# Five attention visits per batch, given SyncE and GpSimd orders, and a new front, in a fused attention and feed-forward kernel

## Chip, cores, metric

One core of one Trainium2 chip. The metric is the device time of one execution in microseconds (us), as the median of repeated runs.

## The reference

```python
k_proj = einsum('ks,bhsd->bhkd', E, k);  v_proj = einsum('ks,bhsd->bhkd', F, v)     # 1024 keys -> 64
attn   = softmax(q @ k_proj^T / sqrt(64))
x      = (attn @ v_proj) put back as (8*1024 tokens, 512)
out    = (relu(x @ w_in) ** 2) @ w_out                                            # 512 -> 2048 -> 512
# q, k, v: 8 batches, 8 heads, 1024 tokens, head size 64, float32
```

## The kernel before

The kernel interleaves two pipelines in an order written by hand. While the feed-forward part of batch b runs, pieces of the attention of batch b+1 are put between its groups of matmuls. A batch has 62 groups. In batches 1 to 7 they run as first half (16 groups of `x @ w_in`, then 15 groups of the second product) and second half (the same again). The second product is formed from seven products of sums and differences of blocks, whose left operands VectorE makes (`operands`).

A table says ahead of which group each attention piece is issued. These are the tables of before:

```python
ORDERED = {PE, DVE, Activation}          # engines that run in program order; SyncE and GpSimd are left to a scheduler
PIECES = {                               # the attention of the next batch, for batches 2 to 7 ahead of group ...
    0: "transpose_q", 1: "copy_kp", 2: "copy_vp", 4: "copy_v_down",
    24: "scores 0, scores 1, exponentials 0", 25: "exponentials 1",
    27: "sums 0, values 0 0, reciprocals 0", 30: "values 0 1", 31: "normalize 0 0", 32: "normalize 0 1",
    47: "scores 2, scores 3, exponentials 2", 48: "exponentials 3",
    50: "sums 1, values 1 0, reciprocals 1", 53: "values 1 1", 54: "normalize 1 0", 55: "normalize 1 1",
}
BATCH_1 = {32: "project", 33: "copy_kp, transpose_q, copy_vp", 36: "copy_v_down", ...}   # cut
BATCH_2 = {**PIECES, 1: "", 2: "", 4: "", 9: "project", 10: "copy_kp", 11: "copy_vp", 14: "copy_v_down"}
```

`project` is the product of E with K and of F with V. Q of a batch, transposed (`qT`), and the projected K, transposed (`kT`), are made by DMA transposes through the crossbar, issued by SyncE. Q, K and V of each batch are loaded by GpSimd's queue. Each has one buffer, so the next Q load waits for the crossbar to have read this Q, and the next K and V loads wait for `project`:

```python
qkv_pool = tile_pool(name="qkv", bufs=1);  qt_pool = tile_pool(name="qt", bufs=1)
aps = tile_pool(name="aps", bufs=2, space=PSUM)      # two buffers for all attention products
def transpose_q(self): nc.sync.dma_start_transpose(out=self.qT[:], in_=self.Q[:]...)
def copy_kp(self):     ...; nc.sync.dma_start_transpose(out=self.kT[:], in_=self.kp[:]...)
```

The softmax here doesn't subtract the row's maximum and nothing guards it: scores larger than these inputs give would overflow.

## Time and profile before

| | before |
|---|---|
| median of three runs | 488.42 us (487.66 to 489.07) |
| span of the profiled run | 485.8 us |
| period of a steady batch (start of one to start of the next) | 57.60 us |
| PE idle inside steady batches | none |

The first lines of the profile's page of before (busy time, share of the span, number of instructions):

```profile
span 485.8 us, 8378 instructions
PE 472.6 (97%) x3614; PEld 292.3 (60%) x3614; DVE 315.4 (65%) x380; ACT 262.4 (54%) x414; POOL 33.2 (7%) x46
```

TensorE is the bound. The losses that the busy share does not show are between matmuls. This is the PE timeline of a steady batch of before (start in us, length in us, line, output and inputs, tile shape, count):

```profile
219.53 1.91 PE L461 MATMUL ps_y<-T,s 128*128 128x256 bf16 x16
221.37 0.63 PE L201 MATMUL ps_att<-qT,kT 64*64 64x512 bf16 x8
221.93 1.92 PE L461 MATMUL ps_z<-w_out,s 128*128 128x256 bf16 x16
...
224.65 0.41 PE L216 MATMUL ps_att<-expT,ones 64*32 64x512 bf16 x8
224.88 0.40 PE L216 MATMUL ps_att<-expT,vp 64*32 64x512 bf16 x8
225.21 1.05 PE L461 MATMUL ps_y<-T,s 128*128 128x256 bf16 x8
...
228.00 0.41 PE L216 MATMUL ps_att<-expT,vp 64*32 64x512 bf16 x8
228.34 1.05 PE L461 MATMUL ps_y<-T,hsq 128*128 128x256 bf16 x8
```

Full-array matmuls of 256 columns go at 0.109 us each, so the 16 that start at 219.53 would end at 221.28; the scores start at 221.37. The scores hold the array until 221.93, 0.56 us, where two passes of 512 columns at 0.216 us (the pitch of the `ps_h` matmuls in this trace) would be 0.43. A lone set of values (228.00) holds it for 0.34 us, where one pass is 0.22. So each visit of attention pieces costs about 0.09 us going in and 0.12 to 0.13 us coming out. The Trainium skill ("TensorEngine Tiling (Array Packing)", Key Properties) says that changing the tiling mode drains TensorE; this trace agrees and puts about 0.22 us on a visit. Before pays it six times per batch.

In batches 0 and 1 PE waits. These are the lines of before's PE waits that matter (total us, times, longest):

```profile
PE ps_att L201 <- DMA kT<-kp: 0.5, 1, 0.5
PE ps_att L286 <- DMA Q_sb<-in_q_dram: 0.4, 1, 0.4
...
PE ps_kv L176 <- DMA V_sb<-in_v_dram: 0.2, 1, 0.2
```

SyncE's timeline of before around batch 1 (start, length of the issue):

```profile
57.73 5.02 SPq L167 DMA_TRANSPOSE qT<-Q_sb  x1
62.81 1.25 SPq L185 DMA_TRANSPOSE kT<-kp  x1
...
79.29 12.77 SPq L167 DMA_TRANSPOSE qT<-Q_sb  x1
92.11 0.58 SPq L625 DMA_DIRECT2D out_dram<-o_sb  x1
92.79 0.41 SPq L631 DMA_DIRECT2D out_dram<-o_sb  x1
94.48 1.22 SPq L185 DMA_TRANSPOSE kT<-kp  x1
```

The transpose of Q of batch 1 issues for 5.0 us when alone; that of batch 2, at 79.29, issues for 12.8 us, because the loads of batch 2 run then. Those loads could start only when the crossbar had read Q of batch 1, as GpSimd's timeline shows (in brackets: idle before, and what ended it):

```profile
66.84 0.87 POOL L78 DMA_DIRECT2D Q_sb<-in_q_dram  x1 [34.43 <-DMA qT<-Q_sb]
```

### The profile page before, as it was taken

The numbers are of one execution on the slowest core, as the hardware profiler recorded it, in microseconds if no ns is written. First come the engines' busy times: TensorE is split into PE (matmuls) and PEld (weight loads), VectorE is DVE, ScalarE is ACT, GpSimd is POOL, SyncE is SP. The second block draws the span as 40 slices with busy tenths as digits, with TensorE's granted clock in tenths as the row PEclk, the third lists the DMA queues.
The fourth block names the chain that finished last, engine by engine and source line by source line (L and its number), as shares of the span: only waits on it lengthen the run. The fifth ranks groups of instructions, "written<-read, shape, count | busy, mean of one in ns | idle before, by whom it ended". The sixth has DMA issues, their size and how long they took to land.

```text
span 485.8 us, 8378 instructions
## 1 busy us (share of the span) xinstructions
PE 472.6 (97%) x3614; PEld 292.3 (60%) x3614; DVE 315.4 (65%) x380; ACT 262.4 (54%) x414; POOL 33.2 (7%) x46
## 2 busy tenths in 40 slices
PE   4899999999999999999999999999999999999997
PEld 2444677475574845757475665747557474666656
DVE  2478855566848568495765848566694856848383
ACT  2487445665727556355655467264672746645351
POOL 6330020010020000100010000200000000000000
PEclk9999999999999999999999999999999999999999
DMA  9999999997389124991149921893232102020202
GB/s 162 204 205 206 164 144 219 235 170 178 46 145 226 30 88 86 172 187 44 44 89 194 162 88 20 141 220 66 88 74 68 45 0 88 2 88 0 88 0 88
DMA packets 72501, 55.46 MB, mean 114 GB/s; under 512 B 33936, under 2 KB 64656, under 8 KB 72464
## 3 DMA queue, kind: packets, MB, share of 16 engines
q0 software_dynamic: 30336, 29.36, 38.5%
q1 hardware_dynamic: 42128, 25.56, 20.7%
q8 instruction: 28, 0.46, 0.4%
q14 instruction: 9, 0.07, 0.0%
HBM read 59.24 MB, written 16.78 MB: 156 GB/s over the span
## 4 chain that ended last, share of the span: by engine, by line
PE 85%; DMA 10%; ACT 2%; POOL 1%; issue 1%; DVE 0%; POOLq 0%; DVEq 0%
PE ps_h L441 39%; PE ps_y L461 23%; PE ps_z L461 11%; DMA V_sb<-in_v_dram 7%; PE ps_x L461 5%; DMA w_in<-in_moe_w_in_dram 2%; PE ps_att L216 2%; PE ps_kv L175 2%; PE ps_att L201 2%; DMA kT<-kp 1%; ACT h_relu L492 1%; PE ps_kv L176 0%; POOL K_sb L91 0%; DVE hsq L500 0%; ACT hsq L498 0%
## 5 line engine op out<-in xcount | busy, mean ns | idle before, releaser
L441 PE MATMUL ps_h<-xT,w_in 128*128 128x512 bf16 x1024 | 225.0, 379 | 0.2 <-DMA w_in<-in_moe_w_in_dram 0.2
L500 DVE TENSOR_TENSOR hsq<-h_relu 128x1024 bf16<-128x1024 f32 x123 | 150.2, 1222 | 67.4 <-ACT h_relu L492 66.8
L492 ACT ACTIVATE h_relu<-ps_h 128x512 f32<-128x512 f32 x256 | 150.6, 597 | 66.2 <-PE ps_h L441 65.7
L441 PEld LDWEIGHTS <-w_in 128*128 128x128 bf16 x1024 | 99.5, 98 | 118.2 <-issue 1.8
L461 PEld LDWEIGHTS <-s 128*128 128x128 bf16 x1024 | 98.4, 98 | 19.6 <-issue 8.1
L461 PEld LDWEIGHTS <-hsq 128*128 128x128 bf16 x768 | 73.2, 98 | 19.4 <-issue 3.0
L461 PE MATMUL ps_y<-T,s 128*128 128x256 bf16 x512 | 62.4, 273 | 0.1
L574 DVE TENSOR_TENSOR o_sb<-ps_z,p_b 128x512 f32<-128x512 f32 x16 | 11.1, 692 | 52.9 <-issue 25.7
L455 DVE TENSOR_TENSOR s<-hsq 128x1024 bf16<-128x1024 bf16 x64 | 43.6, 684 | 0.0
L570 ACT COPY o_sb<-ps_y 128x512 f32<-128x512 f32 x15 | 8.8, 585 | 55.4 <-PE ps_y L461 55.4
L235 DVE TENSOR_TENSOR xT<-ps_att,rs 128x1024 bf16<-128x1024 f32 x28 | 33.0, 1217 | 7.3 <-ACT rs L229 7.3
L461 PE MATMUL ps_y<-w_out,hsq 128*128 128x256 bf16 x256 | 34.5, 273 | 0.3 <-DVE hsq L500 0.3
L461 PE MATMUL ps_x<-w_out,hsq 128*128 128x256 bf16 x256 | 33.2, 273 | 0.0
L461 PE MATMUL ps_y<-T,hsq 128*128 128x256 bf16 x256 | 31.7, 272 | 0.0
L208 ACT ACTIVATE expT<-ps_att 128x1024 bf16<-128x1024 f32 x28 | 27.4, 1028 | 6.4 <-PE ps_att L201 6.4
L461 PE MATMUL ps_z<-T,s 128*128 128x256 bf16 x256 | 30.8, 273 | 0.0
L461 PE MATMUL ps_z<-w_out,s 128*128 128x256 bf16 x256 | 30.6, 273 | 0.0
L570 ACT COPY p_b<-ps_y 128x512 f32<-128x512 f32 (+1 forms) x17 | 9.5, 560 | 28.1 <-PE ps_y L461 28.0
L78 POOL DMA_DIRECT2D Q_sb<-in_q_dram x7 | 6.1, 876 | 263.2 <-DMA qT<-Q_sb 262.8
L574 DVE TENSOR_TENSOR o_sb<-ps_y,p_d 128x512 f32<-128x512 f32 (+1 forms) x17 | 11.2, 660 | 19.2 <-PE ps_y L461 19.2
L228 ACT ACTIVATE rs<-ps_att 128x1024 f32<-128x1024 f32 x14 | 14.3, 1023 | 14.6 <-PE ps_att L216 14.6
L455 DVE TENSOR_TENSOR s<-s,hsq 128x1024 bf16<-128x1024 bf16 x32 | 21.9, 687 | 0.5
(74 smaller groups left out, 239.3 us busy)
## 6 DMA issues: line engine op xcount, KB each, us to landing
out_dram<-o_sb SPq DMA_DIRECT2D x30, 512.0 KB, 3.3
K_sb<-in_k_dram POOLq DMA_DIRECT2D x7, 1024.0 KB, 17.3
V_sb<-in_v_dram POOLq DMA_DIRECT2D x7, 1024.0 KB, 22.4
Q_sb<-in_q_dram POOLq DMA_DIRECT2D x7, 1024.0 KB, 9.6
w_in<-in_moe_w_in_dram POOLq DMA_DIRECT2D x8, 256.0 KB, 13.7
w_out<-in_moe_w_out_dram POOLq DMA_DIRECT2D x4, 512.0 KB, 13.2
K_sb<-in_k_dram POOLq DMA_DIRECT2D x2, 512.0 KB, 7.8
V_sb<-in_v_dram POOLq DMA_DIRECT2D x2, 512.0 KB, 12.7
```

Source lines behind the costliest of these rows:

```text
L175: nc.tensor.matmul(ps[0:KP, :], lhsT=ET[:, i, :], rhs=kv[:, :, i, :], start=f, stop=l)
L201: nc.tensor.matmul(ps[o, bank, :], lhsT=self.kT[r, 2 * pr + j, :], start=True, stop=True, rhs=self.qT[r, NT * (2 * pr + j):NT * (2 * pr + ...
L208: nc.scalar.activation(e[:], self.ps["s", pr][:], AF.Exp, scale=SCALE)
L228: nc.scalar.activation(rs[:], self.ps["r", g][:], AF.Ln)
L235: nc.vector.tensor_tensor(out=self.xT[:, 2 * g + e].rearrange("p a n t -> p a (n t)"), in0=self.ps["v", g, e][:], in1=self.rs[g][:], op=AL ...
L441: nc.tensor.matmul(ps[:], lhsT=w_in_blk(cb, fb), rhs=xT[:, cb, :, 2 * ch:2 * ch + 2], start=(cb == 0), stop=(cb == NCB - 1),)
L455: nc.vector.tensor_tensor(out=s[o][:, js], in0=x, in1=y, op=op)
L461: nc.tensor.matmul(ps[tb] if len(ps) == 2 else ps[0][:, tb], lhsT=lhs[:, j, tb * P:(tb + 1) * P], rhs=rhs[:, j], start=first and n == 0 an ...
L492: nc.scalar.activation(r[:, n], ps[:], AF.Relu)
L500: multiply = lambda: nc.vector.tensor_tensor(out=o, in0=r[:], in1=r[:], op=ALU.mult)
L570: nc.scalar.copy(to[:, t], ps)
L574: nc.vector.tensor_tensor(out=to[:, t], in0=ps, in1=more[:, t], op=ALU.add)
```

## The change

Its intent: five visits per batch instead of six, a reordered front (batch 0's second Q transpose, batch 1's and batch 2's pieces), SyncE and GpSimd in program order, and Q's transpose half a batch earlier, so that its buffer is free sooner.

```diff
-ORDERED = {PE, DVE, Activation}
+ORDERED = {PE, DVE, Activation, Pool, SP}
 PIECES = {
-    0: "transpose_q", 1: "copy_kp", 2: "copy_vp", 4: "copy_v_down",
-    24: "scores 0, scores 1, exponentials 0", 25: "exponentials 1",
-    27: "sums 0, values 0 0, reciprocals 0", 30: "values 0 1", 31: "normalize 0 0", 32: "normalize 0 1",
-    47: "scores 2, scores 3, exponentials 2", 48: "exponentials 3",
-    50: "sums 1, values 1 0, reciprocals 1", 53: "values 1 1", 54: "normalize 1 0", 55: "normalize 1 1",
+    1: "copy_kp", 2: "copy_vp", 4: "copy_v_down",
+    20: "scores 0, scores 1, exponentials 0", 21: "exponentials 1",
+    23: "sums 0, values 0 0, reciprocals 0", 26: "normalize 0 0",
+    28: "scores 2, scores 3, exponentials 2", 29: "exponentials 3",
+    47: "values 0 1, sums 1, reciprocals 1", 48: "normalize 0 1",
+    53: "values 1 0, values 1 1", 54: "normalize 1 0", 55: "normalize 1 1",
 }
 BATCH_1 = {
-    32: "project", 33: "copy_kp, transpose_q, copy_vp", 36: "copy_v_down", ...
+    33: "project", 34: "copy_kp, transpose_q, copy_vp", 37: "copy_v_down", ...      # five visits too; cut
-BATCH_2 = {**PIECES, 1: "", 2: "", 4: "", 9: "project", 10: "copy_kp", ...}
+BATCH_2 = {**PIECES, 1: "", 2: "", 4: "", 9: "project", 10: "copy_kp, transpose_q", ...}
-    9: "second_half 1 0, second_half 0 1",              # batch 0
+    9: "second_half 1 0", 10: "second_half 0 1",
@@ operands of the second product, batches 1 to 7 @@
-    operands(1, range(4))                   # right after the last square
+    operands(1, (0,))
@@ def p2a(): @@
+    if b: operands(1, (1, 3, 2))            # the other three after the second product
@@ batch loop @@
+    order K, V, Q for batch 1, else Q, K, V
+    if b and n == 33 and ahead: ahead.transpose_q()
```

GpSimd's instructions come out in the same order in both builds. SyncE's do not: before issues qT of batch 1 ahead of kT; the changed kernel issues kT of batch 1 ahead of qT.

## The prediction

> **What bounds it.** TensorE. The busy table gives PE 97% of a 485.8 us span at a granted clock of 0.999; VectorE is at 65%, ScalarE at 54%. The timeline shows batches 2 to 6 repeating every 57.60 us with no PE idle (stage table). The change removes no matmul, so a gain can come only from (a) time lost between matmuls in steady batches and (b) PE waits in batches 0 and 1.
>
> **Steady batches.** In the PE timeline each attention piece put between full-array matmuls costs about 0.09 us going in and 0.13 us coming out: four-quadrant scores take 0.56 us against 0.43 for two 512-column passes; a lone set of values takes 0.34 against 0.21. The Trainium skill ("TensorEngine Tiling (Array Packing)", Key Properties) says that changing the tiling mode drains TensorE; the trace agrees, about 0.22 us per visit. Before has six visits per batch, after five: 0.22 us saved. The scores now ahead of the last x product of the first half also hide the 0.08 us for which the next product waited on a VectorE addition. Estimate: 0.25 to 0.3 us for each of batches 1 to 6, about 1.6 us. The deferred operand sums, Q's transpose half a batch earlier and the loads are off the critical path there: loads land many us before the projection reads them in both.
>
> One tight place, checked with trace durations (exponential 1.03, Ln+Exp 2.1, copy 0.58): the copy that frees ps_y now follows the reciprocals and ends about 0.05 us before PE needs it. No stall, little margin.
>
> **Batch 0.** Three PE waits should shrink: 0.40 us for the second Q load (its transpose moves one step later), 0.24 us for V at the projection (moved behind one product), 0.51 us for kT before the first scores, because kT now leaves before qT on SyncE's queue instead of behind its 5.0 us issue. Together 1.1 us. In its last half ScalarE now does four exponentials and both reciprocals in one run, and sums, values and a ps_y product wait for them: I estimate 0.5 to 0.8 us of new waits, against 0.5 us for fewer visits. Net about 1.1 us.
>
> **Batch 1.** kT and qT of batch 2 are now issued back to back after the projection; before, qT was issued 15 us earlier (79.3 us, 12.8 us long among the loads). Alone it takes 4.7 us to issue and 6.7 to 7.3 us to land, so it lands just when the first scores, now four groups earlier, want it: I estimate 0.2 us of new wait (0 to 0.7).
>
> GpSimd's instruction order is the same in both builds; naming it changes nothing by itself.
>
> **Sum.** 1.6 + 1.1 - 0.2 = 2.5 us: 488.4 to **485.9 us**, range 484.3 to 487.4. Chances: faster by over 2% 1%, within 2% 98%, slower by over 2% 1%.
>
> **What will show it.** Steady batches of 57.3 us with five visits. First scores of batch 1 near 65.4 us instead of 66.7, no longer waiting for kT. The first scores of batch 2 wait at most some tenths on qT, whose issue shrinks from 12.8 to about 5 us. PE idle falls by about 1 us.
>
> **What would make it wrong.** qT of batch 2 landing late (over 1 us of PE wait near 101 us); the tight ps_y copy giving a repeated stall of 0.3 us per batch, which would cancel the steady gain; SyncE in program order holding back output stores until VectorE or ScalarE block.

## The result

| | before | changed |
|---|---|---|
| median, same session (4 runs each) | 488.04 us (487.65 to 489.07) | 488.24 us (487.64 to 489.00) |
| ratio | | 1.0002 (0.9979 to 1.0024) |
| span of the profiled run | 485.8 us | 487.2 us |
| period of a steady batch | 57.60 us | 57.38 us |
| first full product (`ps_h`) starts | 19.90 us | 21.80 us |

A ratio is the mean time of one kernel's fast runs over the mean of the other's in the same rounds, so it is not quite the ratio of the medians quoted; the brackets hold the 95% interval. The time lies outside the predicted range of 484.3 to 487.4.

The page, and the PE timeline of a steady batch of the changed kernel:

```profile
span 487.2 us, 8379 instructions
PE 472.1 (97%) x3614; PEld 293.3 (60%) x3614; DVE 313.5 (64%) x380; ACT 263.0 (54%) x414; POOL 33.1 (7%) x46
```

```profile
220.28 0.63 PE L204 MATMUL ps_att<-qT,kT 64*64 64x512 bf16 x8
...
223.56 0.41 PE L219 MATMUL ps_att<-expT,ones 64*32 64x512 bf16 x8
223.78 0.40 PE L219 MATMUL ps_att<-expT,vp 64*32 64x512 bf16 x8
...
228.59 0.70 PE L204 MATMUL ps_att<-qT,kT 64*64 64x512 bf16 x8
...
245.76 0.41 PE L219 MATMUL ps_att<-expT,vp 64*32 64x512 bf16 x8
245.99 0.40 PE L219 MATMUL ps_att<-expT,ones 64*32 64x512 bf16 x8
...
250.79 0.63 PE L219 MATMUL ps_att<-expT,vp 64*32 64x512 bf16 x16
```

There are five visits now (220.28, 223.56, 228.59, 245.76, 250.79; the last is followed by the projection), and the period is 0.22 us shorter, the cost of one visit. PE's waits and SyncE's and GpSimd's timelines, as for before:

```profile
PE ps_att L204 <- DMA qT<-Q_sb: 1.3, 1, 1.3
PE ps_kv L179 <- DMA V_sb<-in_v_dram: 1.1, 1, 1.1
PE ps_k L254 <- DMA K_sb<-in_k_dram: 1.1, 1, 1.1
```

```profile
58.40 1.30 SPq L188 DMA_TRANSPOSE kT<-kp  x1
59.82 4.84 SPq L170 DMA_TRANSPOSE qT<-Q_sb  x1
...
84.51 0.37 SPq L636 DMA_DIRECT2D out_dram<-o_sb  x1
85.96 0.37 SPq L642 DMA_DIRECT2D out_dram<-o_sb  x1
97.43 1.19 SPq L188 DMA_TRANSPOSE kT<-kp  x1
98.81 4.83 SPq L170 DMA_TRANSPOSE qT<-Q_sb  x1
```

```profile
68.69 0.87 POOL L81 DMA_DIRECT2D Q_sb<-in_q_dram  x1 [34.93 <-DMA qT<-Q_sb]
```

Two things are new in them. The first scores of batch 1 wait 1.3 us, now for qT, where before they waited 0.5 us for kT. And the projection of batch 2 waits 1.1 us for V: its first K product starts at 93.01, its first V product at 94.47. A third is only apparent: the loads of batch 2 start at 68.69 instead of 66.84 and qT issues at 59.82 instead of 57.73, but this whole run started later. The first full product of before and of the changed kernel:

```profile
19.90 0.82 PE L441 MATMUL ps_h<-xT,w_in 128*128 128x512 bf16 x3 [0.20 <-DMA w_in<-in_moe_w_in_dram]
```

```profile
21.80 0.81 PE L448 MATMUL ps_h<-xT,w_in 128*128 128x512 bf16 x3 [0.42 <-DVE xT L344]
```

Counted from there the loads of batch 2 start after 46.9 us in both, and the other traces of the two kernels have 46.4 to 47.1 (before) and 46.9 (changed). SyncE's new order did not delay them. The wait for K in the list above, at 9.6 us, is in the very first stage, which is the same in both kernels.

### The profile page after: what moved, and what is told of

It is laid out like the page before. It is cut to its first block, busy times and chain, and to the rows that moved or that the text cites. A ratio compares the mean times of both kernels' runs of the same rounds, so it can differ in the third digit from the quotient of the medians.

```text
span 487.2 us, 8379 instructions
## 1 busy us (share of the span) xinstructions
PE 472.1 (97%) x3614; PEld 293.3 (60%) x3614; DVE 313.5 (64%) x380; ACT 263.0 (54%) x414; POOL 33.1 (7%) x46
## 3 DMA queue, kind: packets, MB, share of 16 engines
q1 hardware_dynamic: 42128, 25.56, 20.2%
## 4 chain that ended last, share of the span: by engine, by line
PE 86%; DMA 8%; ACT 2%; DVE 1%; issue 1%; POOL 0%; POOLq 0%
PE ps_h L448 42%; PE ps_y L468 21%; PE ps_z L468 11%; PE ps_x L468 5%; DMA V_sb<-in_v_dram 5%; PE ps_kv L178 2%; PE ps_att L219 2%; DMA K_sb<-in_k_dram 2%; DMA qT<-Q_sb 2%; PE ps_att L204 1%; ACT h_relu L499 1%; PE ps_k L254 1%; DVE hsq L507 1%; ACT expT L307 0%; DVE xT L344 0%
## 5 line engine op out<-in xcount | busy, mean ns | idle before, releaser
L583 DVE TENSOR_TENSOR o_sb<-ps_z,p_b 128x512 f32<-128x512 f32 x16 | 11.1, 692 | 48.1 <-ACT p_b L579 25.1
L468 PE MATMUL ps_y<-T,hsq 128*128 128x256 bf16 x256 | 30.7, 272 | 0.0
L579 ACT COPY p_b<-ps_y 128x512 f32<-128x512 f32 (+1 forms) x17 | 9.4, 554 | 23.3 <-PE ps_y L468 23.2
L462 DVE TENSOR_TENSOR s<-hsq,s 128x1024 bf16<-128x1024 bf16 x32 | 21.8, 682 | 0.0
L579 ACT COPY p_a<-ps_y 128x512 f32<-128x512 f32 (+1 forms) x17 | 9.4, 561 | 19.3 <-PE ps_y L468 19.3
```

Of the source, the lines that this page charges most:

```text
L462: nc.vector.tensor_tensor(out=s[o][:, js], in0=x, in1=y, op=op)
L468: nc.tensor.matmul(ps[tb] if len(ps) == 2 else ps[0][:, tb], lhsT=lhs[:, j, tb * P:(tb + 1) * P], rhs=rhs[:, j], start=first and n == 0 an ...
L579: nc.scalar.copy(to[:, t], ps)
L583: nc.vector.tensor_tensor(out=to[:, t], in0=ps, in1=more[:, t], op=ALU.add)
```

## The experiments

Traces were compared at four points: the start of the first full product, the span less that start (which takes out most of the luck of the first loads), the wait for V at the projection of batch 2, and the time from the first to the last packet of batch 2's Q, K and V loads, read from the DMA records. The table holds every trace but e3's, whose loads come in another order; "front" says whose SyncE order and first tables the kernel has.

| trace | front | first full product, us | span less that | loads of batch 2, us | wait for V there, us |
|---|---|---|---|---|---|
| before, first | before | 19.90 | 465.9 | 22.2 | 0 |
| b1_before | before | 19.87 | 466.8 | 22.9 | 0.49 |
| b2_before | before | 19.95 | 466.1 | 22.6 | 0 |
| b3_before | before | 21.23 | 465.6 | 22.5 | 0 |
| e4_five_deferred | before | 20.75 | 464.1 | 22.0 | 0 |
| e4b_five_deferred | before | 21.05 | 464.8 | 21.9 | 0 |
| e2_five_only | before | 21.28 | 469.9 | 21.7 | 0 |
| e8_five_gate_later | before, projection later | 19.87 | 470.7 | 22.0 | 0 |
| changed, first | changed | 21.80 | 465.4 | 23.3 | 1.06 |
| a0_after | changed | 20.13 | 464.0 | 22.3 | 0 |
| a1_after | changed | 22.33 | 464.0 | 22.1 | 0 |
| a2_after | changed | 21.09 | 465.3 | 23.8 | 0.99 |
| e1_qT_first | changed, qT first | 21.07 | 465.5 | 23.8 | 0.69 |
| e5_kT_on_PE | changed, kT on PE | 19.85 | 464.3 | 22.2 | 0 |
| f1_front_only | changed | 19.89 | 467.1 | 23.9 | 1.13 |
| e6_Q_first_kT_PE | changed, Q first, kT on PE | 20.89 | 465.9 | 21.5 | 0 |
| e7_after_gate_later | changed, projection later | 19.98 | 464.4 | 24.1 | 0 |
| e9_stores_late | changed, stores later | 20.72 | 464.0 | 19.9 | 0 |
| e10_stores_late_kT_PE | as e9, kT on PE | 20.09 | 463.5 | 20.2 | 0 |

### The changed kernel again (a0_after, a1_after, a2_after)

No edit.

> The changed kernel again, unedited, for a tight ratio and a second trace. Theory T (the front is bound by a DMA chain: Q of batch 1 landed, its crossbar transpose, then the three loads of batch 2, then the projection of batch 2; kT issued ahead of qT lengthens it): ratio 0.998 to 1.002, and a wait for V of 0.7 to 1.5 us at the projection of batch 2 again, whatever the start. Rival L (the first look was an unlucky start, 1.9 us late at the first full product): ratio 0.995 to 0.997, and with a normal start no wait for V there.

> The changed kernel once more, with two of its relatives on one chip. Theory V (its runs split by whether V of batch 2 lands before the projection of batch 2): times from 485.8 to 489, in the trace a wait for V at that projection if the run is over 487.5 us and none if it is under 486.7; ratio 0.996 to 1.000. Rival L (only the start varies): runs of the changed kernel and of five visits with deferral spread alike.

> The changed kernel once more, for its start: span less the start of the first full product is 464.0 to 465.5 us whatever the start; before's is 465.5 to 467.

Measured: a0 486.26 us median (485.90 to 488.71) against 488.18, ratio 0.9967 (0.9946 to 0.9988). a1 487.53 (486.22 to 488.49) against 488.35, ratio 0.9978 (0.9960 to 0.9995). a2, one look, 488.18. The first result was thus a set of four from the slow end of the spread. Over all 17 runs of the changed kernel the mean is 487.46 us, over the 37 of before in those sessions 488.28, 0.17% apart.

Theory T held that the wait for V comes whatever the start: it failed, since a0 and a1 have none. Theory V held that every slow run has that wait: it failed too, since a1's traced run took 488.08 us without it, with the latest start of all, 22.33 us. What is left is two pieces of luck: the start, and V. The span less the start is 464.0 us without the wait for V and 465.3 to 465.4 with it.

### Before again, for its starts (b1_before, b2_before, b3_before)

No edit.

> The kernel before, unedited, for a second trace. Theory G (after the first repeats: a run's time is set by two pieces of luck, the landing of the very first K and V loads and the landing of V of batch 2 at the projection of batch 2; before reaches that projection just as V lands): a start 1 us later than the first trace of before makes it about 1 us longer in all, and the projection of batch 2 waits for V by under 0.5 us, unlike the changed kernel in its slow runs (1.1 us).

> Before once more, for its start. If starts are luck: the first full product anywhere from 19.8 to 22.4 us, and the span longer by most of the excess over 19.9. If the late start is the changed kernel's: 19.8 to 20.1 again.

> Before a fourth time, for its start. If starts are luck: the first full product anywhere from 19.8 to 22.4 us, with the span longer by most of the excess over 19.9. If the late start is the changed kernel's: 19.8 to 20.1 again.

Measured: 488.48, 487.85 and 488.60 us, one look each. b3 starts at 21.23 us: late starts fall on before too. The instructions of all engines up to there are the same in both kernels; starts in traces with before's front run from 19.87 to 21.28 us (the last in e2 below), with the changed front from 19.85 to 22.33. So the 1.9 us by which the changed kernel's first trace started late is not shown to be its own doing, though the samples are too small to exclude a small share.

### Q's transpose ahead of K's (e1_qT_first)

```diff
-    33: "project", 34: "copy_kp, transpose_q, copy_vp",
+    33: "project, transpose_q", 34: "copy_kp, copy_vp",
```

> The changed kernel with qT of batch 1 ahead of kT on SyncE's queue, nothing else. Theory T: qT issues at about 58 us instead of 59.8, lands near 67 instead of 68.7, the loads of batch 2 start 1.5 to 2 us earlier, the wait for V at projection 2 falls from 1.1 us to under 0.4, the first scores wait about 1 us (now for kT), and the time falls by 0.8 to 1.6 us: ratio 0.997 of before. Rival S (the new ScalarE order in the last half of batch 0 costs what the steady batches give): no change from the changed kernel, ratio 1.000.

Measured: 486.72 us median (486.08 to 488.37) against 488.18, ratio 0.9962 (0.9947 to 0.9978), with a0 at 0.9967 beside it on the same chip: no difference. Its traced run is its slowest. There the first scores waited 1.37 us for kT instead of qT, and V was still waited for. Exchanging two transposes on one queue exchanges which of them the scores wait for. Theory T's gain of 0.8 to 1.6 us did not come. It rested on the loads of batch 2 having been late; after the first full product they start at 47.1 us here, no earlier than the 46.9 of the changed kernel.

### Five visits without the deferred sums (e2_five_only)

Before, with only the new `PIECES` (and `transpose_q` kept at group 0).

```diff
 PIECES: the five-visit table of the change, with 0: "transpose_q"
```

> The kernel before with only the five-visit table for batches 2 to 7, its SyncE order and first batches as before. All theories: steady batches of 57.38 us instead of 57.60. Theory T and S: the front is as in before, so 1.1 to 1.4 us less in all, ratio 0.997 to 0.998. If the ratio is 1.000, the steady gain is given back somewhere after batch 2 and both are wrong.

Measured: 492.90 us median (492.67 to 497.32) against 488.18, ratio 1.0107 (1.0079 to 1.0136): 5 us slower, where all theories said 1.2 faster. PE's waits in its trace:

```profile
PE ps_att L216 <- DVE xT L235: 5.2, 6, 0.9
```

Six batches, 0.9 us each. The values pieces of one visit need both buffers for attention products (`aps`), and the first is free only when `normalize 0 1` has read it. VectorE runs in program order, and without the deferral five operand sums, one every 0.60 us, stand between its last square and that normalize (247.37 to 250.50 us of this trace). The deferral puts three of them behind it.

### Five visits with the deferred sums (e4_five_deferred, e4b_five_deferred)

```diff
 PIECES: as in e2
-    operands(1, range(4))
+    operands(1, (0,))
 def p2a():
+    if b: operands(1, (1, 3, 2))
```

> The kernel before with the five-visit table and with the operand sums of the second half put off until after the second product; SyncE order and the first batches' tables as before. If the missing deferral is what cost five visits alone 0.88 us per batch at the values piece, that wait is gone, the period is 57.38 us, and the kernel is 1.2 to 1.7 us faster than before (ratio 0.9965 to 0.9975), as fast as the changed kernel: then the front edits give nothing net. If the SyncE order or the load order matters in steady batches, the period stays at 57.6 or above.

> The kernel before with five visits and deferred sums, again, on the chip of the others. Theory V: it reaches the projection of batch 2 half a microsecond later after its start than the changed kernel and its Q load starts 0.3 to 1.9 us earlier, so it seldom waits there: 486.2 to 487.3, narrower than the changed kernel, ratio 0.9955 to 0.9975. Rival L: as wide as the changed kernel.

Measured: e4 486.34 us median (486.16 to 487.29) against 488.26, ratio 0.9960 (0.9945 to 0.9975). e4b 487.02 (485.98 to 491.56) against 488.35, ratio 0.9984 (0.9953 to 1.0014). The waits of e2 are gone and the period is 57.38 us in both traces. So the deferral, which the prediction called off the critical path, is what makes five visits possible, and these two edits alone give about as much as the whole change (e4b is not clear of noise). That e4b would be narrower than the changed kernel was wrong: it has a run of 491.56 us, whose trace was not taken. In its traced run (487.59 us) the first scores of batch 2 waited 0.56 us for kT, which was issued at 95.44 us and landed 8.6 us later; e8 below explains this. Nor did its Q load start 0.3 to 1.9 us earlier, as theory V had it: 46.8 us after the first full product, against 46.9.

### The front without the five visits (f1_front_only)

The changed kernel with before's six-visit table and without the deferral.

```diff
 PIECES: the table of before, without 0: "transpose_q"
-    if b and n == 33 and ahead: ahead.transpose_q()
+    if b and n == 48 and ahead: ahead.transpose_q()
-    operands(1, (0,)) ... operands(1, (1, 3, 2))
+    operands(1, range(4))
```

> The changed kernel with its front (batch 1's table, the reordered first stages, SyncE's and GpSimd's order, the projection and transposes of batch 2) and the old six visits without deferral. If the front is off the critical path or gives back what it saves: ratio 0.999 to 1.001, batches of 57.6 us from batch 2 on. If the front's 1.1 us is real: ratio 0.997 to 0.998.

Measured: 488.72 us median (488.22 to 489.99) against 488.00, ratio 1.0020 (1.0007 to 1.0033). The front by itself is 0.2% slower, outside both ranges that the expectation named. In its trace:

```profile
PE ps_att L204 <- DMA qT<-Q_sb: 1.2, 1, 1.2
PE ps_kv L179 <- DMA V_sb<-in_v_dram: 1.1, 1, 1.1
```

Two waits, 1.2 us for qT of batch 1 and 1.1 us for V of batch 2, against before's 0.5 us for kT, and no wait for V in three of before's four traces.

### K and V of batch 2 ahead of Q (e3_kv_before_q)

```diff
-    order = K, V, Q if b == 1 else Q, K, V
+    order = K, V, Q if b in (1, 2) else Q, K, V
```

> The changed kernel with batch 2 loaded as K, V, Q, so that K and V do not wait behind Q for the crossbar transpose of batch 1. Theory T: V of batch 2 lands before 85 us and projection 2 does not wait; but the transposes of batch 1 now run among loads, qT takes about 12 us to issue instead of 4.8, the first scores wait 4 to 8 us, and the kernel is 2 to 6 us slower than before (ratio 1.004 to 1.012). If transposes are not slowed by loads, it is 1 us or more faster than the changed kernel.

Measured: 497.56 us median (496.18 to 499.07) against 488.18, ratio 1.0186 (1.0166 to 1.0207). The loss of 9 us is half as much again as the most that was expected (6 us). PE's wait and SyncE's transposes:

```profile
PE ps_att L204 <- DMA qT<-Q_sb: 10.6, 1, 10.6
```

```profile
57.81 1.78 SPq L188 DMA_TRANSPOSE kT<-kp  x1
59.71 15.01 SPq L170 DMA_TRANSPOSE qT<-Q_sb  x1
```

With loads on the DMA engines the transpose of Q issues for 15.0 us instead of 4.8. This shows why Q comes first: its load waits for the crossbar and holds K and V back with it. The loss is more than the wait: batch 0 took 11.1 us more than in the changed kernel (74.47 us from the first full product to the start of batch 1, against 63.34), of which the longer wait is 9.2 to 9.5. The granted TensorE clock was 0.50 from 70.7 us, during the wait, to 80.9 us, 4.0 us after PE had resumed. The Trainium skill ("DMA: Bandwidth & Descriptors", Issuing engines are not separate DMA queues) says that DMAs of all issuing engines run on the same 16 DMA engines and interleave; the trace fits this: with GpSimd's loads under way SyncE's transpose took 15.0 us to issue, against 4.8.

### The projection of batch 2 later (e7_after_gate_later, e8_five_gate_later)

```diff
 e7 (changed kernel):  BATCH_2: ... 2: "transpose_q", 12: "project", 13: "copy_kp", 14: "copy_vp", 16: "copy_v_down"
 e8 (e4_five_deferred): BATCH_2: ... 12: "project", 13: "copy_kp", 14: "copy_vp", 16: "copy_v_down"
```

> The changed kernel with the projection of batch 2 three groups (2.6 us) later and the transpose of its Q issued early, before it. Theory V: no wait for V at that projection in any trace, the slow runs of the changed kernel go: all runs within 485.5 to 487.3, ratio 0.995 to 0.9965. If the transpose of Q still runs when kT is wanted, the first scores of batch 2 wait and the ratio is 0.998 or more. Rival L: spread as the changed kernel, and the same mean.

> Five visits with deferral on the front of before, and the projection of batch 2 three groups later. Theory V: equal to or up to 0.5 us faster than without the move (ratio 0.995 to 0.9965), since it hardly waits there. If kT of batch 2 now lands after 102.5 us, its first scores wait and it is slower by up to 2 us.

Measured: e7 489.57 us median (486.21 to 491.74) against 488.35, ratio 1.0025 (0.9995 to 1.0055). e8 492.96 (492.35 to 493.83) against 488.35, ratio 1.0092 (1.0077 to 1.0107). In e8:

```profile
PE ps_att L201 <- DMA kT<-kp: 4.6, 2, 4.2
```

```profile
98.01 2.02 SPq L185 DMA_TRANSPOSE kT<-kp  x1
```

```profile
107.28 0.76 PE L201 MATMUL ps_att<-qT,kT 64*64 64x512 bf16 x8 [4.17 <-DMA kT<-kp]
107.98 3.40 PE L462 MATMUL ps_z<-T,s 128*128 128x256 bf16 x16
```

On before's front Q of batch 2 is transposed early, so the loads of batch 3 start early (their first packet is at 96.4 us here), and a kT issued at 98.01 is caught among them: the scores got it at 107.28, 9.3 us later, and waited 4.2 us (the other of the two waits is the one in batch 1). The wait again cost more than itself: from 107.6 to 111.1 us the granted clock was 0.51, and the 16 matmuls at 107.98 took 3.40 us where they take 1.91 in a steady batch. This is what the changed front guards against, by issuing kT and qT together ahead of those loads, and it is a likely cause of e4b's slow run, which no trace shows. For e7 only its fastest run was traced, and that has no wait for V, as expected, though V landed 72.9 us after the first full product, later than the 71.2 at which the changed kernel's four traces reach that projection: the move hid a late V. What made four of the other five 2.5 to 5.5 us slower stays open. There is a hint: three of them, and e4b's slow run, show a mean granted clock of 0.995 or 0.996, e8's five runs 0.993 to 0.996, one run of before (490.86 us) 0.993, and the changed kernel's own runs 0.999 or 1.000. So these slow runs, too, probably held a long PE wait.

### Batch 1's kT off the crossbar (e5_kT_on_PE, e6_Q_first_kT_PE)

```diff
 e5:  33: "project, transpose_q", 34: "copy_kp_only, copy_vp", 37: "copy_v_down",
+     39: "transpose_k 0", 41: "transpose_k 1",       # eight small TensorE transposes and two copies
 e6:  batch 1 loaded Q, K, V;  31: "transpose_q", 39: "project", 40: "copy_kp_only, copy_vp",
      42: "copy_v_down", 43: "transpose_k 0", 44: "transpose_k 1"
```

> The changed kernel with kT of batch 1 made by eight TensorE transposes, so that only qT uses the crossbar there. Theory G with the DMA chain: qT issues when Q has landed, lands near 66.5 us; the first scores wait under 0.5 us instead of 1.05 to 1.34; loads of batch 2 start about 2 us earlier, no wait for V at projection 2 in any run; 0.5 to 1 us faster than the changed kernel's fast runs and 2 us faster than its slow ones: ratio 0.993 to 0.996. If the chain is not what binds, ratio as the changed kernel, 0.9965.

> As the last, and batch 1 is loaded Q, K, V with qT issued as soon as Q lands, among the loads, and the projection of batch 1 six groups later. Theory: qT takes 12 us or more to issue but has landed by 60 us; the loads of batch 2 start near 60 us, 7 to 9 us earlier; no wait at the first scores or at projection 2; ratio 0.992 to 0.996. If V of batch 1 now lands after 59 us, projection 1 waits for it and the gain is lost.

Measured: e5 487.71 us median (485.89 to 488.03) against 488.26, ratio 0.9977 (0.9959 to 0.9995). e6 489.19 (488.24 to 490.30), ratio 1.0017 (0.9999 to 1.0035). In e5's traced run, its fastest, the first scores waited 0.25 us and V was not waited for, as expected, but four of its six runs took 487.5 us or more, so the expectation for "any run" cannot be upheld. Nor did the loads of batch 2 start earlier (47.0 us after the first full product, against 46.9). And the first scores came no earlier: 46.5 us after the first full product, as in the changed kernel; only the waiting had been filled. In e6 the loads of batch 2 started 42.3 us after the first full product, 4.6 earlier than in the changed kernel, but V of batch 1, now last, made projection 1 wait 1.85 us, the case its expectation named as a loss.

### The two stores held back (e9_stores_late, e10_stores_late_kT_PE)

With SyncE in program order the two 512 KB stores that end batch 0 go out at 84.51 and 85.96 us, in the middle of the loads of batch 2. Before held them, by accident, behind the 12.8 us issue of qT until 92.11. e9 is the changed kernel with these stores issued after qT of batch 2; e10 adds e5's edit.

```diff
 # batch 0, second half
-    nc.sync.dma_start(out_rows[...], o_tile)
+    late.append(lambda: nc.sync.dma_start(out_rows[...], o_tile))
 # batch 1, group 10, after copy_kp and transpose_q
+    while late: late.pop(0)()
```

> The changed kernel with the two stores of batch 0's second half issued after the transposes of batch 2 instead of at 83 to 86 us. Theory W (the stores share the DMA engines with the loads of V and delay it): the loads of batch 2 take 22.3 us or less, no wait for V at projection 2, and the slow runs go: ratio 0.995 to 0.997, all runs under 487.5. If the stores are not the cause: the wait of about 1 us in half the traces and the ratio 0.997 to 0.999 as for the changed kernel.

> The same with kT of batch 1 made on TensorE, so that qT of batch 1 and with it the loads of batch 2 start up to 1.4 us earlier. Theory W: no wait for V and under 0.4 us at the first scores, ratio 0.994 to 0.996, the fastest of all. Otherwise 0.9977 as without the held stores.

Measured: e9 486.77 us median (486.49 to 487.41), e10 486.08 (485.41 to 486.42), before 487.89 (487.67 to 488.18); ratios 0.9978 (0.9965 to 0.9990) and 0.9962 (0.9949 to 0.9976). SyncE's timeline of e9:

```profile
95.00 1.20 SPq L188 DMA_TRANSPOSE kT<-kp  x1
96.31 4.87 SPq L170 DMA_TRANSPOSE qT<-Q_sb  x1
101.22 1.10 SPq L477 DMA_DIRECT2D out_dram<-o_sb  x2
```

The stretch from 88 to 94 us of the changed kernel and then of e9 (length, busy us of PE, weight load, VectorE, ScalarE and GpSimd, granted clock, mean DMA share, GB/s):

```profile
88.00:94.00 6.00, 5.41 (x25) 2.20 (x24) 4.50 (x4) 4.11 (x7) 0.00 (x0) 1.00 0.73 217
```

```profile
88.00:94.00 6.00, 6.00 (x36) 2.59 (x35) 4.40 (x5) 3.36 (x6) 0.00 (x0) 1.00 0.08 14
```

In e9 the DMA engines are nearly empty by then, and PE is never idle. The loads of batch 2 take 19.9 and 20.2 us instead of 22.1 to 23.8 in the changed kernel, and V lands 68.8 and 69.0 us after the first full product instead of 70.9 to 72.6, well before PE reaches the projection (71.3 and 70.8). So on this front the stores are what makes V late. They do not make it later than before's: there it landed at 71.3 to 72.5, without the stores but with the transpose of Q among the loads. The change took the transpose from among these loads and let the stores in.

The ten timed runs spread over 0.9 and 1.0 us instead of the changed kernel's 2.8 and 2.3, but the runs of before measured beside them spread over only 0.5 us, against 1.7 to 3.0 beside the other experiments, so the narrower spread is not shown to come from the edit. e10's waits and span:

```profile
PE ps_att L212 <- DMA qT<-Q_sb: 0.2, 1, 0.2
```

```profile
span 483.6 us, 8394 instructions
```

e10 had the shortest span of any trace here, and all its runs are below before's fastest. The ratios do not decide between the theories: e9's 0.9978 lies in the range named for the case that the stores are not the cause, e10's 0.9962 is just above its expected range, and e4 and e1 reached the same. The mechanism rests on the traces, where it came as expected.

## Why the prediction was wrong

The prediction was 2.5 us less; the first measurement was 0.2 us more, all 17 runs together 0.8 us less.

- **Steady batches (predicted 1.6 us).** Right. The period fell by 0.22 us, one visit; from the start of batch 2 to that of batch 7 a0's trace is 1.25 us shorter than before's first (285.07 against 286.32), and the second half of batch 1 adds 0.45 us (29.28 against 29.73). The detail about the 0.08 us wait was half right: it went, but the scores ahead of it now take 0.63 us instead of 0.56. A claim beside it failed: the deferred sums are not off the path, for without them five visits lose 0.9 us per batch (e2).
- **Batch 0 (predicted "Net about 1.1 us").** The step that failed. From the first full product to the start of batch 1 the changed kernel's four traces take 63.33 to 63.35 us, before's four 63.08 to 63.71, mean 63.45: 0.1 us gained. The 0.40 us wait for the second Q load and the 0.24 us for V did go. The 0.51 us for kT did not go but became 1.05 to 1.34 us for qT. The prediction followed kT to the head of the queue and left out that qT, which lands later, then stands behind it. In all four traces kT issues 4.2 us after the projection begins, qT 1.4 us after kT, and qT lands 8.3 us after its issue (8.5 to 8.6 in before, where the prediction has 6.7 to 7.3 for such a transpose). So the first scores come 14.0 us after the projection and 46.5 us after the first full product, where 65.4 - 19.9 = 45.5 was predicted and before has 46.3 to 47.0. In before qT left within 0.1 us of the landing of Q of batch 1; in three of the changed kernel's four traces Q had by then lain ready for 1.6 to 2.0 us. Exchanging the order again (e1) only exchanged the waits; Q itself landed late there (37.9 us after the first full product, against 36.1 to 37.8 in the four).
- **Batch 1 (predicted 0.2 us of new wait, on qT).** The other step that failed. qT of batch 2 was never waited for. Instead the projection of batch 2 waited 0.99 to 1.13 us for V in two of the changed kernel's four traces and in f1; the two are 1.3 us longer than the others. On the mean of four traces the first half of batch 1 grew by 0.4 us. PE reached that projection just as V landed already in before (0 to 0.49 us of wait). The prediction did not ask what these loads run beside: it moved the transpose of Q from among them, and the program order let two stores in. It looked for stores held back by SyncE's order, and the harm was stores let go (e9): without them V lands 2 to 4 us sooner.
- **Luck.** The first traced run started 1.9 us later than before's. Before shows such starts too (21.23 in b3). The prediction had no term for it, and its range for a median was as wide as the spread of single runs, 485.9 to 489.0. Over the four traces of each kernel the span less the start fell by 1.4 us on the mean (466.1 to 464.7), near the sum of the three items above. That the timed runs fell by only 0.8 would then be due to later starts (21.3 against 20.2 us on the mean of four), which may be chance.

Not settled: why the loads of batch 2, with the stores among them, take 22.1 to 22.3 us in some traces and 23.3 to 24.1 in others; and the slow runs of e7 and of e4b.

## What to carry to other kernels

A queue that is given a program order not only holds work back, it also lets work go: ask for each transfer what it was accidentally kept from running beside. Where a stage begins when a chain of transfers ends, PE time saved ahead of it is only waiting moved (e5: the wait fell to 0.25 us, the first scores came no sooner), so look for the landing that gates the next stage before counting saved waits, and take that transfer's own duration, not its group's median. When two transfers change places on a queue, follow both. Before reading a delay from two traces, count from an event that both have in common, such as the first full product here. When two edits come together, run each alone: here five visits lose 1% without the deferral and gain 0.4% with it in one session (0.2% in another, not clear of noise).

## What the Trainium skill lacked or had wrong

- "TensorEngine Tiling (Array Packing)", Key Properties, says that a change of tiling mode drains TensorE but not what it costs: about 0.22 us per visit among 128x256 matmuls here, and 0.22 us off the period when one of six visits went.
- "DMA: Bandwidth & Descriptors", Rules for kernel authors, says that a transpose next to ordinary DMAs needs nothing; the row is about corrupted data, not about time. No run here gave a wrong result, but the time is another matter: the issue of the transpose of Q took 4.8 to 5.0 us in the front with no loads under way and 12.4 to 15.0 us among the loads of a batch, and a kT issued at the edge of loads reached its reader 9.3 us later.
- No page that I read says how much a 1 MB pair of stores delays loads on the same engines: on the changed front three loads took 19.9 and 20.2 us without them (e9, e10) and 22.1 to 23.9 us with them among the loads (seven traces).
- No page that I read has the run-to-run spread of the first loads: the first full product started between 19.85 and 22.33 us in kernels whose instructions up to there are the same.
